# Two H3 convolution layers and two MLP layers on one core: the skip weight D added by TensorE, one more channel group turned by DMA, LayerNorm statistics swapped between VectorE and ScalarE, and a new order of the front

## The chip, the cores and the metric

The kernel runs on one core of a Trainium2 chip. A core has five engines with their own in-order instruction queues: TensorE (PE in the profile; PEld is its weight load), VectorE (DVE), ScalarE (ACT), GpSimd (POOL) and SyncE (SP), which here issues nearly all DMAs. They meet only at semaphores. Matmuls write to PSUM; VectorE and ScalarE copy PSUM to SBUF (an *evacuation*), while GpSimd works on SBUF alone. The metric is the device time of one execution in microseconds. Before the change the median of three runs was 256.5 us (255.91 to 257.84).

## The reference, cut to what matters

```python
def _A_ref(q, k, v, shift_k, ssm_k, ssm_D):          # S = 2048 tokens, D = 512 channels
    k_shift = sum(k_pad[:, t:t + S, :] * shift_k[:, ks - 1 - t] for t in range(4))   # four taps
    kv = k_shift * v
    y = irfft(rfft(kv, 2 * S) * rfft(ssm_k, 2 * S))[:, :S, :].astype(bf16)  # long causal convolution
    return q * (y + kv * ssm_D)                      # D: a skip weight for each channel
def _B_ref(x, w1, b1, w2, b2):                       # MLP 512 -> 1376 -> 512
    return gelu(layernorm(x) @ w1 + b1) @ w2 + b2

x = A_q
x = x + _A_ref(layernorm(x), ...);  x = x + _B_ref(layernorm(x), ...)
x = x + _A_ref(layernorm(x), ...);  x = x + _B_ref(layernorm(x), ...)
```

Both A layers use the same k, v and kernels, and only their gate q differs, so the convolution `y + kv * D` is computed once and used twice. Adding D to the first sample of the convolution kernel gives the same result as `kv * D`: this is how the kernel does it.

## The kernel before, in words

The program has a **front** (to about 98 us in the profile), which computes the convolution for all tokens and the first token group's gate, and an **MLP part** of eight rounds (two layers of four token groups), each a product with w1 and Gelu (`mm1`, lines 704 and 706) and a product with w2 (`mm2`, line 738).

The front is a list of pieces. Each piece is planned with `plan.add` and names its dependences, and the string ORDER at the head of the file fixes the order by hand: a word such as `U2S0.P02` is a piece, its engine (P TensorE, A ScalarE, D VectorE, G GpSimd, S SyncE) and the buffers that it takes. Each engine runs its pieces in the order of that string. There are four PSUM buffers p0 to p3 (of 1024 f32 columns each), three SBUF buffers ZT, three xb and three T.

The pieces, by channel group cc = 0 to 3 of 128 channels (a trailing `e` is the evacuation of the piece before it):

- **lk, lv, lK, lX, lW, lM, lx0, lx1, lx**: loads of k, v, the convolution kernel, tables, and of the input x. lx0 and lx1 are token groups 0 and 1 for LayerNorm 0; lx is all of x once more, into the place of v.
- **kT**: k turned by TensorE (line 441). **dg**: diagonal matrices of the tap weights (line 435), which the matmuls **kv** (line 524) use to apply the four taps for cc 0 to 2; **kvm** multiplies by v on VectorE (line 530). For cc = 3 the taps are **kg** and **ka** on GpSimd (lines 455 to 462, about 4 us each), and kgm.
- **kd**: D is added to the first sample of the convolution kernel, `Kd[:, :, 0] += Dz`, on VectorE (line 393), once for each half of it.
- **KS, K2** (lines 400 and 413): the transform of the convolution kernel in two stages of 16 pieces each.
- **US** (line 325): first transform stage of u = kv, four pieces for each cc. **UT**: u is turned between its stages, in two halves, by 16 transposes on TensorE and an evacuation (line 357), or by a DMA transpose (line 304), as the string `UT` says for each cc.
- **X, T, V** (lines 558, 573, 582): 16 rounds of second stage, product with the kernel's transform (VectorE, 128x2048) and first inverse stage. A T needs KSW, a rearranged copy of K2's result that the loads **sa** and **sb** make.
- **Z, TC, TD** (lines 629, 617): the result turned again, by DMA for cc 0 and 1 and by TensorE for cc 2 and 3. **Y** (line 649): last inverse stage for each token group. **g0, h0, p0, b0** (lines 674, 259, 271, 276): gate, statistics, root and scaling for group 0's three units (tokens 0, 1 and 2 to 3 of the group). **LT0** (line 657): its first unit turned for mm1.
- **s0, s1, s02**: LayerNorm 0's statistics for groups 0 and 1 (on VectorE lines 259 to 268, on ScalarE lines 487 to 490), their scale on GpSimd, and group 0's scaling (line 508).

Behind the front, PSUM's place is taken over by the tiles `ph` (four, where p0 and p1 were) and `po` (four, where p2 and p3 were) of the MLP part.

Of the kernel before, what the change touches and what calls it, by code (L numbers as in the profile page):

```python
# [11 lines left out]
ALU = mybir.AluOpType  # L12
# [18 lines left out]
T20.D0 X21e.A U3S1.P1 U0T0.P2 lx.S U3S1e.A T10.D1 X13.P30 U3S3e.A V20.P10 U0T0e.D X13e.A U3T0.S X23.P01 T21.D2
U0T1.P2 V20e.A T13.D0 X00.P32 X23e.A V10.P11 U0T1e.D X00e.A V21.P0 V10e.A T23.D1 X01.P30 V13.P2 V21e.A T00.D2
# [93 lines left out]
def kernel(ctx: ExitStack, tc: tile.TileContext, A_q, A_k, A_v, A_shift_k, A_ssm_k, A_ssm_D,  # L126
                 B_x, B_w1, B_b1, B_w2, B_b2, out):
    nc = tc.nc
    P = 128
    _, S, D = A_q.shape  # L130
    F = B_w1.shape[1]
# [3 lines left out]
    FT = (F + P - 1) // P  # L135
    FL = F - (FT - 1) * P
# [98 lines left out]
    def evac(eng, dst, src):  # L235
        if eng == "A":
            nc.scalar.activation(dst, src, AF.Copy)  # L237
        else:
            nc.vector.tensor_copy(dst, src)  # L239
# [587 lines left out]
```

## Time and profile before

| what | us |
|---|---|
| median of three runs | 256.5 |
| the profiled execution's own time | 256.8 |
| its span (all that the profile shows) | 255.1 |
| TensorE busy in the span | 236.8 |
| VectorE / ScalarE busy in the span | 174.5 / 146.1 |
| GpSimd busy in the span | 54.5 |

The profile gives one execution. Time that lies outside the span (256.8 - 255.1 = 1.7 us) is not seen in it. In its rows, the first number is the start in us from the span's start, the second the length; `x4` means four instructions merged into a row; in brackets stand the idle time of the engine just before, and what ended it. Busy shares are averages over stages that have different limits, so each stage is read for itself. Merged rows overlap a little, since an instruction starts before the one ahead of it has drained: a copy shown with 1.22 us follows the last one after 1.16.

### The profile page before, as it was taken

The page shows a single profiled execution, that of the slowest core. Times are in us where ns is not written, and L with a number is a line of the kernel's source. Part 1 is how long each engine was busy: PE and PEld are TensorE (multiplying, and loading weights), DVE is VectorE, ACT ScalarE, POOL GpSimd, SP SyncE. Part 2 cuts the span into 40 slices and gives each one's busy share as a digit, 9 for nine tenths or more (in the row PEclk, how much of TensorE's full clock was granted, in tenths as well). Part 3 has the DMA queues.
Part 4 walks back from the last instruction along what each step waited for, and adds up shares of the span by engine and source line. Part 5 has one row for each costly group of instructions (what it writes and reads, how often), then busy time and mean ns, then how long its engine had stood idle before and what let it go on. Part 6 is the DMA issues. An engine that isn't in the chain of part 4 may idle for free.

```text
span 255.1 us, 5088 instructions
## 1 busy us (share of the span) xinstructions
PE 236.8 (93%) x2084; PEld 146.3 (57%) x2084; DVE 174.5 (68%) x321; ACT 146.1 (57%) x210; POOL 54.5 (21%) x52
## 2 busy tenths in 40 slices
PE   1898479999999999999999999999999999999995
PEld 0698446889989857854444444444444444444443
DVE  0345988899999897787889989886866863022022
ACT  3698388899999799921821721722712712812810
POOL 2499999310000011011110111110110110000000
PEclk9999975899999999999999999999999999999999
DMA  5999994199967898004040401304006006002001
GB/s 132 382 334 167 222 442 180 76 320 321 312 135 103 148 237 288 3 0 82 5 82 0 78 6 20 62 0 82 4 1 165 0 11 157 0 14 71 1 20 63
DMA packets 53040, 30.15 MB, mean 118 GB/s; under 512 B 46642, under 2 KB 50456, under 8 KB 51736
## 3 DMA queue, kind: packets, MB, share of 16 engines
q1 hardware_dynamic: 52864, 29.73, 43.5%
q8 instruction: 16, 0.26, 0.4%
q10 hardware_dynamic: 152, 0.09, 0.1%
q14 instruction: 8, 0.07, 0.1%
HBM read 16.71 MB, written 2.10 MB: 74 GB/s over the span
## 4 chain that ended last, share of the span: by engine, by line
PE 72%; DVE 12%; DMA 7%; issue 4%; ACT 2%; SPq 2%; ACTq 0%; DVEq 0%
PE po L738 30%; PE ph L704 29%; DMA arena<-in_A_v_dram 4%; DVE T L573 4%; DVE arena L239 3%; PE p L325 2%; PE p L357 2%; PE p L649 2%; DVE arena L393 2%; DMA arena<-in_A_ssm_D_dram 2%; PE p L400 2%; PE p L413 2%; PE p L524 1%; DVE ZT L239 1%; DMA arena<-ZT 1%
## 5 line engine op out<-in xcount | busy, mean ns | idle before, releaser
L706 ACT ACTIVATE arena<-ph,B 128x512 bf16<-128x512 f32 (+5 forms) x110 | 63.7, 604 | 81.1 <-PE ph L704 81.0
L704 PE MATMUL ph<-arena 128*128 128x512 bf16 (+4 forms) x440 | 78.5, 336 | 0.1
L738 PE MATMUL po<-arena 128*128 128x512 bf16 (+2 forms) x363 | 77.4, 373 | 0.0
L704 PEld LDWEIGHTS <-arena 128*128 128x128 bf16 (+1 forms) x440 | 40.4, 100 | 37.2 <-DMA arena<-in_B_w_dram 0.4
L738 PEld LDWEIGHTS <-arena 128*128 128x128 bf16 (+1 forms) x363 | 35.4, 98 | 40.5
L743 DVE TENSOR_TENSOR arena<-po,arena 128x512 bf16<-128x512 f32 (+1 forms) x33 | 21.5, 673 | 43.6 <-PE po L738 43.6
L237 ACT ACTIVATE arena<-p 128x1024 bf16<-128x1024 f32 (+5 forms) x38 | 37.8, 1071 | 10.1 <-PE p L441 3.9
L271 POOL TENSOR_TENSOR lrsm<-lrsm,mhalf 128x4 f32<-128x4 f32 (+2 forms) x10 | 8.9, 885 | 95.9 <-DVE lrsm L265 95.9
L237 ACT ACTIVATE ZT<-p 128x1024 bf16<-128x1024 f32 (+1 forms) x22 | 22.0, 1055 | 2.5 <-PE p L325 2.5
L259 DVE BATCH_NORM_STATS2 lstm<-arena 128x6 f32<-128x512 bf16 x32 | 19.9, 681 | 0.2
L573 DVE TENSOR_TENSOR T<-xb,arena 128x2048 bf16<-128x2048 bf16 (+1 forms) x17 | 18.7, 1159 | 0.0
L239 DVE CAST arena<-p 128x1024 bf16<-128x1024 f32 x15 | 17.7, 1223 | 1.4 <-PE p L400 0.9
L582 PE MATMUL p<-arena,T 128*128 128x128 bf16 x256 | 16.5, 219 | 1.0 <-DVE arena L239 0.4
L271 POOL TENSOR_TENSOR lrsg<-lrsg,mhalf 128x4 f32<-128x4 f32 x8 | 8.1, 1014 | 40.2 <-DVE lrsg L268 40.1
L237 ACT ACTIVATE xb<-p 128x1024 bf16<-128x1024 f32 x15 | 16.1, 1165 | 0.1
L582 PEld LDWEIGHTS <-T 128*128 128x128 bf16 x256 | 14.9, 98 | 1.6 <-issue 1.3
L455 POOL TENSOR_TENSOR T<-arena,SK 128x2048 bf16<-128x2048 bf16 (+3 forms) x4 | 14.9, 3740 | 3.8 <-ACT arena L237 3.7
L259 DVE BATCH_NORM_STATS2 lstg<-arena 128x6 f32<-128x512 bf16 x24 | 14.8, 679 | 0.0
L276 DVE TENSOR_SCALAR arena<-arena,lmvg,lrsg 128x512 bf16<-128x512 bf16 x28 | 9.7, 409 | 6.7 <-POOL lrsg L271 6.7
L239 DVE COPY arena<-p 128x2048 bf16<-128x2048 bf16 (+3 forms) x10 | 10.5, 1049 | 4.4 <-issue 3.0
L276 DVE TENSOR_SCALAR arena<-arena,lmvm,lrsm 128x512 bf16<-128x512 bf16 x32 | 11.2, 409 | 2.3 <-POOL lrsm L271 2.3
L524 PE MATMUL p<-DG,arena 128*128 128x128 bf16 x192 | 11.4, 219 | 1.2 <-ACT ZT L237 0.9
(73 smaller groups left out, 226.8 us busy)
## 6 DMA issues: line engine op xcount, KB each, us to landing
arena<-arena SPq DMA_DIRECT2D x8, 512.0 KB, 4.2
arena<-in_A_k_dram SPq DMA_DIRECT2D x4, 512.0 KB, 6.2
arena<-in_A_v_dram SPq DMA_DIRECT2D x2, 1024.0 KB, 9.6
arena<-in_A_ssm_k_dram SPq DMA_DIRECT2D x4, 512.0 KB, 7.9
arena<-tabM SPq DMA_DIRECT2D x1, 2048.0 KB, 12.1
arena<-in_A_q_dram SPq DMA_DIRECT2D x1, 2048.0 KB, 8.2
out_dram<-arena SPq DMA_DIRECT2D x15, 128.0 KB, 1.7
arena<-in_B_w_dram SPq DMA_DIRECT2D x1, 1376.0 KB, 6.5
```

The source lines that it names most:

```text
L237: nc.scalar.activation(dst, src, AF.Copy)
L239: nc.vector.tensor_copy(dst, src)
L259: nc.vector.bn_stats(self.st[:, i, 0, :], x_t[:, GT * g + i, :] if src is None else src[:, i, :])
L271: nc.gpsimd.tensor_tensor(self.rs[:, a:b], self.rs[:, a:b], mhalf[:, a:b], ALU.pow)
L276: nc.vector.tensor_scalar(out=dst[:, i, :], in0=xs, scalar1=self.mv[:, i, 0:1], scalar2=self.rs[:, i:i + 1], op0=ALU.subtract, op1=ALU.mult)
L455: nc.gpsimd.tensor_tensor(m[:, t:NT, :], kn[:, 0:NT - t, c3], sk(t, NT - t), ALU.mult)
L573: eng.tensor_tensor(view(Tb[it["slot"]["T"]], [2, n, CW]), x2, kk, ALU.mult)
L582: nc.tensor.matmul(o[:, i, :], T[:, r, i, :], Mt[:, ka + i, 1 - r, :], start=r == 0, stop=r == 1)
L704: nc.tensor.matmul(o.rearrange("p (i t) -> p i t", t=P), W1t[:, ct, ft * P:ft * P + m], lt[:, a:b, ct, :], start=ct == 0, stop=ct == CT - 1)
L706: nc.scalar.activation(hT[0:m, ft, a * P:b * P], o, AF.Gelu_apprx_tanh, bias=B1[0:m, ft:ft + 1])
L738: nc.tensor.matmul(po[:, a:b], hT[0:m, ft, i * P:(i + 1) * P], W2t[0:m, ft, a:b], start=ft == 0, stop=ft == FT - 1)
L743: nc.vector.tensor_tensor(xs, po[:, a:b], xs, ALU.add)
```

## The change

1. **D by TensorE.** kd becomes two matmuls with the identity, `Kd[:, :, 0]` and `Dz` summed in PSUM, and an evacuation of 128x64 back into Kd, which the new order gives to ScalarE.
2. **u of cc = 2 turned by DMA** (`UT` is `PPXX`): U2T0 and U2T1 become DMA transposes.
3. **x in four loads** lr0 to lr3, one for each token group, that wait for all US and for X30 and X31; the first gate waits for lr0 only. lr1 to lr3 stand among the weight loads at the front's end. The weight loads no longer wait for all T: w1 for the first two T of each cc, the others for the second and third.
4. **GpSimd's taps** wait until all three dg are made.
5. **LayerNorm 0**: group 0's scaling s02 may run on ScalarE alone (it did). In the new order group 0's statistics are on VectorE and group 1's on ScalarE; before it was the other way round.
6. **A new ORDER**, with new planned costs. The planned costs have no effect on the program: the order is written out.

```diff
@@ ORDER (only two of its lines)
-lSK.S lk1.S lsT.S lk3.S lk0.S lk2.S bSK.P0 lh1.S bSKe.A lh113.S lx0.S kT1.P1 lv0.S sF.G lv1.S dg0.D dg2.D
+lSK.S lk1.S lk3.S lk2.S lk0.S lsT.S lh1.S lx0.S bSK.P0 lh113.S bSKe.D kT1.P1 lx1.S lv1.S kT3.P2 kT1e.A lv0.S
...
-    UT = "PPPX"
+    UT = "PPXX"
...
-                kd = plan.add(f"kd{c}", {"G": 300, "D": 130}, lK[c * NK // 8], lambda it, sl=sl: (
-                    nc.vector if it["eng"] == "D" else nc.gpsimd).tensor_tensor(Kd[:, sl, 0], Kd[:, sl, 0], Dz[:, sl], ALU.add))
+                def mms(o, sl=sl):
+                    nc.tensor.matmul(o, IDt[:], Kd[:, sl, 0], start=True, stop=False)
+                    nc.tensor.matmul(o, IDt[:], Dz[:, sl], start=False, stop=True)
+                _, kd = mm_evac(f"kd{c}", 120, lK[c * NK // 8], mms, [P // NK], lambda sl=sl: Kd[:, sl, 0])
...
-            kg.append(plan.add(f"kg{t}", {"G": 4650 if t else 4100}, kg[-1:] if t else lk + lS[2:] + [bSK], lambda it, t=t: tap(t)))
+            kg.append(plan.add(f"kg{t}", {"G": 4650 if t else 4100}, kg[-1:] if t else lk + lS[2:] + [bSK] + dg, lambda it, t=t: tap(t)))
...
-            return s0, plan.add("s02", {"D": 1350, "A": 2200}, [s1], apply) if n == 0 else s1
+            return s0, plan.add("s02", {"A": 2900}, [s1], apply) if n == 0 else s1
...
-        lx = load("lx", x_t[:], q_d.rearrange(TOK, p=P), 2 ** 21, USp)
...
-        w1 = load("w1", W1t[:], B_w1.rearrange("(ct p) f -> p ct f", p=P), 1376 << 10, sum(Tcc, []))
-        wd = sum(Tcc, [])
+        lx = [load(f"lr{g}", x_t[:, GT * g:GT * g + GT, :], xd[:, GT * g:GT * g + GT, :], 2 ** 19, USp + Xcc[3][:2],
+                   rank=2 if g else 0) for g in range(4)]
+        w1 = load("w1", W1t[:], B_w1.rearrange("(ct p) f -> p ct f", p=P), 1376 << 10, sum((t[0:2] for t in Tcc), []))
+        wd, we = sum(Tcc, []), sum((t[1:3] for t in Tcc), [])
...
-            ga = plan.add(f"g0{a}", {"D": 1190 if m == 2 else 930}, [y, s2, lx], gate, free=yf)
+            ga = plan.add(f"g0{a}", {"D": 1190 if m == 2 else 930}, [y, s2, lx[0]], gate, free=yf)
```

What the new order does on the engines, at three places. First VectorE, from the first product with v (line 530, now 532) on to the evacuations of KS (`128x64x8x2`). `p0` to `p3` are the PSUM buffers; line 393 is the addition of D. Before:

```order
L530 TENSOR_TENSOR arena_64<-p2_121,arena_64 128x8x128
L239 CAST ZT0_95<-p1_120 128x4x8x32
L393 TENSOR_TENSOR arena_64<-arena_64,Dz_72 128x64
L530 TENSOR_TENSOR arena_64<-p3_122,arena_64 128x8x128
L239 CAST arena_64<-p1_120 128x64x8x2
```

After, from the evacuation of the last kT on (line 259 and the two rows behind it are group 0's statistics):

```order
L239 COPY arena_64<-p0_119 128x4x3x128
L259 BN_STATS lstg0_104<-arena_64 128x6 x4
L263 BN_AGGR lmvg0_105<-lstg0_104 128x2 x4
L268 TENSOR_SCALAR lrsg0_106<-lmvg0_105 128x4
L532 TENSOR_TENSOR arena_64<-p1_120,arena_64 128x8x128
L532 TENSOR_TENSOR arena_64<-p2_121,arena_64 128x8x128
L532 TENSOR_TENSOR arena_64<-p3_122,arena_64 128x8x128
L532 TENSOR_TENSOR arena_64<-p0_119,arena_64 128x8x128
L239 CAST ZT0_95<-p1_120 128x4x8x32
L532 TENSOR_TENSOR arena_64<-p2_121,arena_64 128x8x128
```

The addition of D has left VectorE, and the statistics of group 0 stand ahead of the first product with v.

Second SyncE's queue, from the last copies of KSW (`64x4096`) to the weights; line 304 is the turning of u (ZT1 holds cc = 2, ZT0 cc = 3), line 632 a Z. This is what stands there now:

```order
L301 DMA arena_64<-arena_64 64x4096 x6
L304 DMA_TRANSPOSE arena_64<-ZT1_96 128x16x128
L304 DMA_TRANSPOSE arena_64<-ZT0_95 128x16x128
L304 DMA_TRANSPOSE arena_64<-ZT1_96 128x16x128
L632 DMA_TRANSPOSE arena_64<-arena_64 128x8x128
L304 DMA_TRANSPOSE arena_64<-ZT0_95 128x16x128
L632 DMA_TRANSPOSE arena_64<-arena_64 128x8x128
L301 DMA arena_64<-in_A_q_dram 128x2048
L632 DMA_TRANSPOSE arena_64<-ZT2_97 128x8x128
```

Before, the load of all of x (`128x8192`) followed KSW's copies, then the two turns of cc = 3, and then all Z. Now there are four turns of u with a Z (Z01) ahead of the last one, and x's first quarter stands behind the second Z.

Third VectorE at the end of the front, from the evacuation TC2e (`128x8x256`) to the scaling of group 0's last unit (line 276, x2), behind which the MLP part has it. Before:

```order
L239 COPY arena_64<-p0_119 128x8x256
L276 TENSOR_SCALAR arena_64<-arena_64,lmvm0_111,lrsm0_112 128x512
L674 TENSOR_TENSOR arena_64<-arena_64 128x1024
L675 TENSOR_TENSOR arena_64<-arena_64 128x1024
L276 TENSOR_SCALAR arena_64<-arena_64,lmvm0_111,lrsm0_112 128x512
L239 COPY arena_64<-p0_119 128x512
L259 BN_STATS lstm0_110<-arena_64 128x6 x2
L263 BN_AGGR lmvm0_111<-lstm0_110 128x2 x2
L265 TENSOR_SCALAR lrsm0_112<-lmvm0_111 128x2
L239 CAST arena_64<-p2_121 128x1024
```

After, the last ten rows of that stretch:

```order
L678 TENSOR_TENSOR arena_64<-arena_64 128x1024
L259 BN_STATS lstm0_110<-arena_64 128x6
L263 BN_AGGR lmvm0_111<-lstm0_110 128x2
L265 TENSOR_SCALAR lrsm0_112<-lmvm0_111 128x1
L239 CAST arena_64<-p3_122 128x1024
L276 TENSOR_SCALAR arena_64<-arena_64,lmvm0_111,lrsm0_112 128x512
L259 BN_STATS lstm0_110<-arena_64 128x6 x2
L263 BN_AGGR lmvm0_111<-lstm0_110 128x2 x2
L265 TENSOR_SCALAR lrsm0_112<-lmvm0_111 128x2
L239 CAST arena_64<-p1_120 128x1024
```

VectorE now evacuates two of the last Y there (Y22 from p3 and, last of all, Y12 from p1), where before it was one (Y32 from p2), and LT0 has gone to ScalarE. By the program's semaphores, the first tile of mm1 takes p0's place and the second p1's: before, the second tile waited for ScalarE's evacuation of Y20 out of p1, and now it waits for VectorE's evacuation of Y12.

54 lines of the change are left out of this document (27 added, 27 removed).

## The prediction, made before the changed kernel was run

> **What bounds the kernel now.** I read the busy time by stage first, then the rows in order of time. Columns: stretch, its length, busy us (and instructions) of PE, PEld, DVE, ACT, POOL, then granted clock, DMA share, GB/s.
>
> ```profile
> 60.00:70.00 10.00, 9.91 (x163) 9.59 (x161) 10.00 (x10) 10.00 (x12) 0.00 (x0) 1.00 1.07 295
> 70.00:80.00 10.00, 9.20 (x159) 8.84 (x157) 10.00 (x10) 10.00 (x12) 0.00 (x0) 1.00 0.45 98
> 110.00:255.00 145.00, 142.15 (x669) 65.86 (x667) 88.88 (x212) 52.90 (x78) 13.09 (x13) 1.00 0.18 41
> ```
>
> Behind 110 us TensorE is busy for 142 of 145 us: the MLP part is bound by it, and the change touches nothing there. From 60 to 80 it is VectorE and ScalarE, both at 10.00 of 10, that bound the front, while TensorE has gaps. So a us taken from VectorE ahead of the last T counts; one taken from TensorE there does not. I follow one **anchor**, the first matmul of the product with w2 (109.37, below). The 145.7 us behind it stay, and so do the 1.7 us outside the span: time = anchor + 147.4 us (256.8 for this execution, 0.3 above the median).
>
> **Part 1: to VectorE's first evacuation of K2.** What the added D costs now:
>
> ```profile
> 25.95 3.61 POOL L455 TENSOR_TENSOR T<-arena,SK 128x1792 bf16<-128x1792 bf16 x1
> 26.35 3.52 DVE L393 TENSOR_TENSOR arena<-arena,Dz 128x64 bf16<-128x64 bf16 x1
> 29.93 0.64 PE L400 MATMUL p<-Ft,arena 32*128 32x64 bf16 x32 [2.79 <-DVE arena L393]
> ```
> ```profile
> 34.40 3.37 POOL L455 TENSOR_TENSOR T<-arena,SK 128x1664 bf16<-128x1664 bf16 x1
> 36.35 1.73 DVE L393 TENSOR_TENSOR arena<-arena,Dz 128x64 bf16<-128x64 bf16 x1
> 38.13 0.78 PE L400 MATMUL p<-Ft,arena 32*128 32x64 bf16 x48 [1.58 <-DVE arena L393]
> ```
>
> 64 elements take VectorE 3.52 and 1.73 us, and each ends 0.3 us behind the GpSimd tap that began before it: the addition is held by the tap. TensorE waits 2.79 and 1.58 us for it. The product with v at 15.32 (line 530, one operand in PSUM, below) runs beside a tap at 1.22 and is not held. In the new kernel TensorE adds D and ScalarE evacuates 128x64. No row shows that one:
>
> ```profile
> L237 ACT ACTIVATE arena<-p 128x256 bf16<-128x256 bf16 x2 | 0.8, 383 | 0.4 <-PE p L617 0.3
> L488 ACT ACTIVATE as<-as 128x4 f32<-128x4 f32 x1 | 0.2, 207 | 0.0
> L487 ACT ACTIVATE arena<-arena 128x512 bf16<-128x512 bf16 x4 | 2.5, 630 | 0.2
> L490 ACT ACTIVATE arena<-arena,as 128x512 bf16<-128x512 bf16 x4 | 2.9, 722 | 0.1
> ```
>
> 128x256 took 0.38 us and 128x4 0.21, so 0.2 to 0.4, say 0.3, on ScalarE, and beside it TensorE's two matmuls of 64 columns, under 0.2. Both waits go, 4.4 us of TensorE's. What is late next is VectorE's own queue, so I count from its start:
>
> ```profile
> 11.18 0.98 PEld L441 LDWEIGHTS <-arena 128*128 128x128 bf16 x12 [0.39 <-DMA arena<-in_A_k_dram]
> 11.31 7.95 POOL L455 TENSOR_TENSOR T<-arena,SK 128x2048 bf16<-128x2048 bf16 x2 [3.67 <-ACT arena L237]
> 12.66 3.75 PE L524 MATMUL p<-DG,arena 128*128 128x128 bf16 x64 [0.33 <-ACT arena L237]
> 15.32 1.22 DVE L530 TENSOR_TENSOR arena<-p,arena 128x1024 bf16<-128x1024 f32 x1 [1.93 <-DMA arena<-in_A_v_dram]
> 17.91 2.36 DVE L530 TENSOR_TENSOR arena<-p,arena 128x1024 bf16<-128x1024 f32 x2 [1.36 <-DMA arena<-in_A_v_dram]
> ```
> ```profile
> 10.00:16.00 6.00, 5.54 (x82) 5.11 (x81) 1.63 (x2) 5.72 (x12) 4.69 (x2) 1.00 1.04 407
> ```
>
> kv starts at 12.66 and takes 1.88 each (3.75 for two); the last k landed at 11.2. The little load behind dg now stands behind all four loads of k, and kT0's evacuation stands behind dg0 on VectorE: about 11.5 landed, then cast (0.2), dg0 (0.7) and the copy (1.0) give kv at 13.4, and the four kv ahead of kvm20 end at 20.9. v used to land for 15.32 and 17.91; lx1 now goes ahead, 0.52 MB at 407 GB/s or 1.3 us, so 16.6 and 19.2, hidden behind kv. From 20.9 VectorE has six pieces of 1.23 (three products with v, three US), eight KS at 1.16 and two US, 19.1 us: it is free for K2 at **40.0**. ScalarE has two dg to 14.3, group 1's statistics (lines 487 to 490: 2.5 + 2.9 and the small steps, 6.6 us) to 20.9 and group 0's scaling (2.9) to 23.8, and then waits for kd0 at 25.6: nothing, with a cover of 1.8 us; what goes beyond it delays KS one for one.
>
> Two terms are added. (a) Group 0's statistics now run on VectorE from 13.4 to 16.5, while the first tap, which waits for dg1, runs from about 14.3 to 18.4. Their last step is an SBUF-to-SBUF operation as line 393 was. If held, VectorE begins with v at 18.5 and is 1.2 late at kvm20: 0 to 1.2, I take 0.6. (b) The clock:
>
> ```profile
> 28.93:32.34 3.41, 1.94 (x77) 1.00 0.87 304
> 32.34:35.76 3.42, 3.42 (x44) 0.50 1.08 447
> 35.76:39.17 3.42, 1.57 (x82) 1.00 0.99 422
> 39.17:42.58 3.41, 3.28 (x83) 0.50 0.59 240
> 42.58:46.00 3.42, 3.42 (x24) 0.50 0.00 0
> ```
>
> (Columns: busy PE, granted clock, DMA share, GB/s.) Both times a stretch with only 1.6 to 1.9 us of TensorE work, mostly KS matmuls of 32 rows, was followed by half clock; and a stretch full of KS (39.17) did not end it. KS stays, so I expect half clock again at K2's start, where three US and three K2 must run before VectorE's first one: 0 to 1.7, I take 1.4. Sum: 40.0 + 0.6 + 1.4 = **42.0**, before 46.38.
>
> The Trainium skill (TensorE: Matmul & The Clock Gate, What's actually happening) says that the clock halves after an idle window of some 3.4 us. This trace halves it after windows that were half busy, so the measurement decides; by the rule (b) would be nothing, and the time 1.4 us less.
>
> **Part 2: to the last T.**
>
> ```profile
> L573 DVE TENSOR_TENSOR T<-xb,arena 128x2048 bf16<-128x2048 bf16 x15 | 17.5, 1222 | 0.0
> L239 DVE CAST arena<-p 128x1024 bf16<-128x1024 f32 x6 | 7.1, 1219 | 0.5 <-PE p L413 0.5
> L239 DVE COPY arena<-p 128x2048 bf16<-128x2048 bf16 x5 | 6.1, 1223 | 0.8 <-PE p L357 0.4 <-issue 0.3
> L239 DVE CAST ZT<-p 128x1024 bf16<-128x1024 f32 x3 | 3.7, 1222 | 0.0
> L259 DVE BATCH_NORM_STATS2 lstg<-T 128x6 f32<-128x512 bf16 x4 | 2.5, 679 | 0.0
> ```
> ```profile
> 46.38 1.23 DVE L239 CAST arena<-p 128x1024 bf16<-128x1024 f32 x1 [0.34 <-PE p L413]
> 47.75 4.62 DVE L239 CAST arena<-p 128x1024 bf16<-128x1024 f32 x4 [0.15 <-PE p L413]
> ```
> ```profile
> 79.98 4.70 DVE L573 TENSOR_TENSOR T<-xb,arena 128x2048 bf16<-128x2048 bf16 x5
> ```
>
> From 46.38 to 84.68 (79.98 + 4.70) VectorE spends 38.3 us without a real gap. In the new order group 1's statistics leave (3.1 with their small steps), and of five 128x2048 copies of UT four stay (-1.2); it gets six K2 instead of five (+1.2) and six other casts instead of four (+2.4). Sum -0.7. Laying the 16 rounds out with these durations leaves it 0.4 us of new waits: 42.0 + 38.0 = **80.0**, before 84.68. **So the front's gain is 4.7 us**, and most of it comes from D, not from the turning: the 32 transposes that TensorE saves lie beside a saturated VectorE.
>
> The turning moves to SyncE:
>
> ```profile
> L304 SPq DMA_TRANSPOSE arena<-ZT x2: 3849/4944/6039, 63.6 to 69.7; - x2
> ```
> ```profile
> 87.91 2.70 SPq L629 DMA_TRANSPOSE arena<-ZT  x2
> ```
>
> One half took 3.8 to 6.0 us of the queue, waits for the loads ahead included. At 2.7 (two Z, together as much data, take 2.70) all four end by 70; X32, the tightest, comes at 74.5: cover 4 us. x's four loads and the weights come 10 us ahead of use or more: nothing. w1's earlier release is not used, since it stands behind all Z.
>
> **Part 3: from the last T to the anchor**, before 109.37 - 84.68 = 24.7 us.
>
> ```profile
> 96.87 0.42 DVE L239 COPY arena<-p 128x512 bf16<-128x512 bf16 x1
> 98.81 1.22 DVE L239 CAST arena<-p 128x1024 bf16<-128x1024 f32 x1
> ```
> ```profile
> 97.91 2.11 PE L704 MATMUL ph<-arena 128*128 128x128 bf16 x32
> 100.09 0.38 PE L657 MATMUL po<-IDt,arena 128*128 128x128 bf16 x4
> 109.37 2.97 PE L738 MATMUL po<-arena 128*128 128x512 bf16 x13
> ```
>
> Now VectorE's last evacuation (Y32, out of p2) ends at 100.05, 15.4 behind the last T, and mm1 hardly notices: it has done 8 of 11 tiles of its first unit by then. After the change mm1's *second* tile needs p1, which VectorE empties last (Y12). VectorE's list there gains an evacuation (1.2) and a small one (0.3) and loses LT0's (0.4), but it also loses some 0.9 of waits: Y12 ends at 15.6. TensorE, done with Y12 at about 13, stands still for 2.5 us, and 7 tiles that were done before (0.264 each, 2.11 for 8) come afterwards: 0.2 + 1.85, and 0.15, an estimate, for one more handoff between TensorE and ScalarE. **The tail loses 2.2 us.** Such a pause can halve the clock again (above: half-busy windows): 0 to 1.7, I take 0.8 as it depends on where the window falls.
>
> Sum: anchor 109.4 - 4.7 + 2.2 + 0.8 = 107.7, time **255.1 us**.
>
> **Rivals.** *B, the clock stays full at K2 and at the pause, and nothing of the statistics is held*: for it, much of the KS stage is mixed with US. S is 40.0, so 40.0 + 38.0 - 84.7 + 2.2 = -4.5: **252.3**. *C, the tap holds all of group 0's statistics*, not only their last step: two of four run before 14.3, the rest from 18.4, and VectorE begins with v at 20.4 instead of 16.6. kvm20 is 3.2 late instead of 0.6: 255.1 + 2.6 = **257.7**, slower than before. For it: 3.52 us on line 393. Against it: an operation with one SBUF operand is none that the trace shows held.
> The Trainium skill (GPSIMD Engine Reference, Key points) has GpSimd contend with VectorE operations that have two SBUF inputs or run in a 2-port mode. Line 393 agrees with 3.52 us; statistics with one input would fall under it only in such a mode, which no run here shows.
> *D, SyncE's queue becomes the bound*: at 5 us for each half (the mean of 9.95 for two) U3's second half, which stands behind a Z, lands at 78 instead of 70, and X32 stands still for 3.5 us, and the last T with it: **258.6**; it decides from 3.5 us a half on. *E, TensorE goes on waiting for D*, now for ScalarE's evacuation of it, which stands behind group 0's scaling: the cover is 1.8 us, and if ScalarE is 3 us later than laid out, KS is 1.2 late: **256.3**.
>
> **Chances.** Forecast 0.52, B 0.25, C 0.09, D 0.11, E 0.03. A measurement of this kernel can tell about 1% (2.6 us) from no change. Faster by more: B and a little of the forecast's range, 0.28. Slower by more needs C or D with the clock's full price (1.7 instead of 0.8) or with each other: 0.13. Within: 0.59. The forecast's own range is 253.3 to 257.3 (terms a and b and the pause at their ends). Range: from B, 252.0, to D with the full clock price, 259.4.
>
> **What would show it.** Line 393 gone and no TensorE wait ahead of KS; VectorE's first K2 evacuation at 42 (B: 40, C: 44.6) and the last T at 80; half clock at K2's start; statistics of group 0 that end by 16.5 or 18.6; a pause of 2 to 3 us in mm1 right behind its first tile, ended by VectorE, and the anchor 27 to 28 us behind the last T. The prediction is wrong if mm1 runs without that pause, or if VectorE has gaps of microseconds between K2 and the last T.

## The result, and the profile after

The changed kernel takes **259.2 us** (median of seven runs, 258.13 to 260.03), the kernel before 256.8 in the same comparison: 1.0085 times as long, with a 95% interval of 1.0063 to 1.0106. The prediction was 255.1, range 252.0 to 259.4: forecast a little faster, measured slower by 0.85%. The profiled execution took 258.1 us, the least of the seven, with a span of 256.4. The ratios here leave out executions more than 1.5% above the fastest of the same kernel: three of the six of warm_ks, one of u2_by_pe, and one of the kernel before beside stats_first_only.

Three points divide the span as the prediction did:

| | before | predicted | after (profiled) |
|---|---|---|---|
| VectorE's first evacuation of K2 begins | 46.38 | 42.0 | 44.94 |
| last T ends | 84.68 | 80.0 | 82.27 |
| anchor: first product with w2 | 109.37 | 107.7 | 110.47 |
| from the last T to the anchor | 24.69 | 27.7 | 28.20 |

So the end of the front lost what was forecast (3.5 us instead of 3.0), and the front gained 2.4 us instead of 4.7. The front's loss can be read at its start, in VectorE's rows in order of time (start, length, line, operation, out<-in):

```profile
10.89 0.96 DVE L239 COPY arena<-p 128x1536 bf16<-128x1536 bf16 x1 [7.47 <-PE p L443]
11.76 4.43 DVE L437 TENSOR_SCALAR DG<-IDt,sF 128x128 bf16<-128x128 bf16 x4
16.11 0.94 DVE L239 COPY arena<-p 128x1536 bf16<-128x1536 bf16 x1
16.98 2.45 DVE L259 BATCH_NORM_STATS2 lstg<-arena 128x6 f32<-128x512 bf16 x4
...
19.75 0.17 DVE L268 TENSOR_SCALAR lrsg<-lmvg 128x4 f32<-128x4 f32 x1
19.86 1.22 DVE L532 TENSOR_TENSOR arena<-p,arena 128x1024 bf16<-128x1024 f32 x1
...
24.95 1.22 DVE L532 TENSOR_TENSOR arena<-p,arena 128x1024 bf16<-128x1024 f32 x1 [0.56 <-PE p L526]
```

The four small operations that make the diagonal dg0 take 4.43 us together. The view of that line alone gives each one's shortest, median and longest duration in ns:

```profile
L437 DVE TENSOR_SCALAR DG<-IDt,sF x4: 241/242/3942, 11.8 to 15.9; 128x128 bf16<-128x128 bf16 x4
```

Three took 0.24 us, one 3.94. On GpSimd, in the same stretch:

```profile
11.33 0.20 POOL L382 CAST sF<-sT 128x16 f32<-128x16 bf16 x1 [3.87 <-DMA sT<-in_A_shift_k_dram]
11.56 4.09 POOL L457 TENSOR_TENSOR T<-arena,SK 128x2048 bf16<-128x2048 bf16 x1
```

The first tap began at 11.56, right behind the cast, and **ahead of** the diagonals for which the change was to hold it. It ends at 15.65 (11.56 + 4.09). The four operations begin at 11.76, and the last of them starts at 15.9, so the long one ends with the tap. TensorE waits for dg0:

```profile
15.76 9.15 PE L526 MATMUL p<-DG,arena 128*128 128x128 bf16 x128 [3.32 <-DVE DG L437]
```

and all that VectorE has behind dg0 (the last kT, the statistics, the products with v) comes as much later. Before, VectorE made all three diagonals from 7.67 on, since the load behind them landed earlier, and the first tap began only at 11.31:

```profile
7.67 2.04 DVE L435 TENSOR_SCALAR DG<-IDt,sF 128x128 bf16<-128x128 bf16 x12 [7.67 <-POOL sF L382]
```

The end of the front is as the prediction had it. TensorE's rows (with its wait in brackets), VectorE's last evacuation, and the clock in stretches of 2 us (busy PE, granted clock, DMA share, GB/s):

```profile
94.90 0.39 PE L707 MATMUL ph<-arena 128*128 128x128 bf16 x4
98.04 3.14 PE L707 MATMUL ph<-arena 128*128 128x128 bf16 x28 [2.75 <-DVE arena L239]
```
```profile
96.76 1.23 DVE L239 CAST arena<-p 128x1024 bf16<-128x1024 f32 x1
```
```profile
96.00:98.00 2.00, 0.00 (x0) 1.00 1.07 377
98.00:100.00 2.00, 1.96 (x19) 0.50 1.09 375
100.00:102.00 2.00, 2.00 (x27) 0.65 0.47 172
102.00:104.00 2.00, 1.99 (x33) 1.00 0.02 6
```

One tile of mm1, then 2.75 us of nothing until Y12 has left p1, then half clock for about 3.4 us.

### The profile page after: what moved, and what is told of

Its sections match the earlier page's. It is cut to its first block, busy times and chain, and to the rows that moved or that the text cites. A ratio compares the mean times of both kernels' runs of the same rounds, so it can differ in the third digit from the quotient of the medians.

```text
span 256.4 us, 5044 instructions
## 1 busy us (share of the span) xinstructions
PE 237.8 (93%) x2056; PEld 148.1 (58%) x2056; DVE 178.8 (70%) x318; ACT 141.1 (55%) x211; POOL 54.6 (21%) x52
## 4 chain that ended last, share of the span: by engine, by line
PE 76%; DVE 13%; DMA 5%; ACT 2%; issue 2%; SPq 1%; DVEq 0%; ACTq 0%
PE ph L707 30%; PE po L741 30%; DVE arena L239 5%; PE p L526 4%; DMA arena<-in_A_k_dram 2%; DMA arena<-ZT 2%; PE p L325 2%; PE p L583 2%; DVE ZT L239 2%; PE p L620 2%; PE p L402 2%; DVE T L574 2%; DVE DG L437 2%; PE p L415 1%; DVE arena L532 1%
## 5 line engine op out<-in xcount | busy, mean ns | idle before, releaser
L707 PE MATMUL ph<-arena 128*128 128x512 bf16 (+4 forms) x440 | 80.0, 342 | 2.9 <-DVE arena L239 2.8
L707 PEld LDWEIGHTS <-arena 128*128 128x128 bf16 (+1 forms) x440 | 41.9, 103 | 39.8 <-issue 2.9
L741 PEld LDWEIGHTS <-arena 128*128 128x128 bf16 (+1 forms) x363 | 35.5, 98 | 40.5
L746 DVE TENSOR_TENSOR arena<-po,arena 128x512 bf16<-128x512 f32 (+1 forms) x33 | 21.5, 672 | 43.5 <-PE po L741 43.5
L237 ACT ACTIVATE arena<-p 128x1024 bf16<-128x1024 f32 (+7 forms) x36 | 33.1, 996 | 13.3 <-PE p L394 5.6
L239 DVE CAST arena<-p 128x1024 bf16<-128x1024 f32 x17 | 20.0, 1216 | 1.1 <-PE p L402 0.7
L237 ACT ACTIVATE ZT<-p 128x1024 bf16<-128x1024 f32 (+1 forms) x19 | 18.8, 1034 | 1.1 <-PE p L325 1.1
L259 DVE BATCH_NORM_STATS2 lstg<-arena 128x6 f32<-128x512 bf16 x28 | 17.2, 676 | 0.0
L526 PE MATMUL p<-DG,arena 128*128 128x128 bf16 x192 | 13.1, 234 | 3.3 <-DVE DG L437 3.3
L239 DVE COPY arena<-p 128x2048 bf16<-128x2048 bf16 (+3 forms) x10 | 9.9, 1006 | 8.8 <-PE p L443 7.5
L526 PEld LDWEIGHTS <-arena 128*128 128x128 bf16 x192 | 12.5, 106 | 3.8 <-DVE DG L437 3.6
L237 ACT ACTIVATE xb<-p 128x1024 bf16<-128x1024 f32 x14 | 14.4, 1075 | 0.2 <-PE p L559 0.2
```

The costliest lines, as they stand in the source:

```text
L259: nc.vector.bn_stats(self.st[:, i, 0, :], x_t[:, GT * g + i, :] if src is None else src[:, i, :])
L526: nc.tensor.matmul(o[:, i, :], w, DG[:, cc, t, :], start=t == 0, stop=t == KS - 1)
L707: nc.tensor.matmul(o.rearrange("p (i t) -> p i t", t=P), W1t[:, ct, ft * P:ft * P + m], lt[:, a:b, ct, :], start=ct == 0, stop=ct == CT - 1)
L741: nc.tensor.matmul(po[:, a:b], hT[0:m, ft, i * P:(i + 1) * P], W2t[0:m, ft, a:b], start=ft == 0, stop=ft == FT - 1)
L746: nc.vector.tensor_tensor(xs, po[:, a:b], xs, ALU.add)
```

## The experiments

All times below are compared with the kernel before on the same chip; a median is of 4 to 12 executions (hold_forms: one). K2 is the start of VectorE's first evacuation of K2 in the profiled execution, T the end of the last T, A the anchor.

| run | median us | ratio to before (95%) | K2 | T | A | A - T |
|---|---|---|---|---|---|---|
| after | 259.2 | 1.0085 (1.0063 to 1.0106) | 44.94 | 82.27 | 110.47 | 28.2 |
| tap_waits | 256.9 | 0.9973 (0.9951 to 0.9995) | 44.63 | 81.90 | 109.81 | 27.9 |
| tail_slots | 256.3 | 0.9952 (0.9927 to 0.9976) | 46.85 | 84.08 | 109.14 | 25.1 |
| both_fixes | 253.7 | 0.9853 (0.9818 to 0.9888) | 44.84 | 82.11 | 107.19 | 25.1 |
| before_d_pe | 254.9 | 0.9885 (0.9851 to 0.9918) | 44.33 | 82.75 | 107.45 | 24.7 |
| stats_first | 252.5 | 0.9817 (0.9783 to 0.9851) | 42.65 | 79.88 | 104.93 | 25.1 |
| diag_act | 252.3 | 0.9807 (0.9780 to 0.9834) | 41.50 | 79.24 | 104.32 | 25.1 |
| stats_first_only | 255.2 | 0.9933 (0.9906 to 0.9961) | 42.37 | 79.58 | 107.48 | 27.9 |
| d_on_dve | 257.9 | 1.0024 (1.0005 to 1.0043) | 47.71 | 85.04 | 110.11 | 25.1 |
| u2_by_pe | 257.2 | 0.9996 (0.9964 to 1.0029) | 42.12 | 84.08 | 109.12 | 25.0 |
| v_first | 254.9 | 0.9897 (0.9870 to 0.9924) | 44.98 | 82.27 | 107.37 | 25.1 |
| warm_ks (three of six in the ratio) | 256.7 | 0.9874 (0.9832 to 0.9916) | 48.58 | 85.87 | 110.91 | 25.0 |
| hold_forms | 258.9 | none (one execution) | 48.95 | 86.16 | 111.21 | 25.1 |

The kernel after and tail_slots have the same front, and their K2 stands at 44.94 and 46.85: one execution differs from the next by up to 2 us there. So causes are read from the rows, and prices from the ratios: a difference of 0.01 between two of them is 2.6 us.

### tap_waits: the tap made to wait for the diagonals

```diff
+            if not t:
+                nc.gpsimd.tensor_copy(ksum[:, 0, 0:CK], DG[:, :, KS - 1, 0])
             nc.gpsimd.tensor_tensor(m[:, t:NT, :], kn[:, 0:NT - t, c3], sk(t, NT - t), ALU.mult)
```

> The kernel after, with one 128x3 copy on GpSimd ahead of the first tap that reads the last diagonal of each group, so that the tap really waits for all three. Theory W (in the kernel after nothing made the tap wait: it began at 11.56 beside VectorE's four diagonals, held one of them for 3.94 us, and the product with the taps began at 15.76 where the prediction had 13.4): the four diagonals take about 1 us, the products kv begin at 12.7 to 13.4, VectorE's first evacuation of K2 comes at 42.0 to 42.6 instead of 44.94, and the time falls by 2.4 to 2.9 us from the kernel after, to about 256.5. If the tap, which then runs from 14.1 to 18.1, holds group 0's last statistics step, that step ends at 18.2 and not by 16.5. Rival T (something else made VectorE late there, and the tap only lay beside it): the diagonals stay long, and the time stays within 1 us of the kernel after. Rival Q (the queue of transposes is at its limit already, since X32 waited 0.7 us for one in the kernel after): the first evacuation of K2 comes at 42.3, but the last T moves by less than 1.5 us.

The ratio fell by 0.0112, or 2.9 us. VectorE and GpSimd:

```profile
11.85 0.74 DVE L437 TENSOR_SCALAR DG<-IDt,sF 128x128 bf16<-128x128 bf16 x4 [0.35 <-POOL sF L382]
...
16.15 2.63 DVE L268 TENSOR_SCALAR lrsg<-lmvg 128x4 f32<-128x4 f32 x1
```
```profile
14.64 4.12 POOL L459 TENSOR_TENSOR T<-arena,SK 128x2048 bf16<-128x2048 bf16 x1
```

The diagonals take 0.74 us instead of 4.43: the tap was the cause, and rival T falls. But the tap, moved, now holds the next operation of that kind: four numbers in each partition take 2.63 us, to 18.78, when the tap ends at 18.76. Of the 3.7 us won, VectorE keeps 1.2 at first (it begins with v at 18.70 instead of 19.86) and, since it no longer waits for kv, 2.9 at kvm20 (22.1, the last of four products that take 4.60 us from 18.70, instead of 24.95). Even so K2 moved by only 0.3 between the two profiled executions, not by the 2.4 to 2.9 expected: in this one the clock was 0.70 from 22.10 to 25.50 and 0.80 from there to 28.90, where the kernel after had 1.00, and the 32 matmuls of kv at 22.68 took 2.93 us instead of 1.95. A longer queue of transposes (rival Q) isn't what took it: from K2 to the last T it took 37.27 us, as in the kernel after (37.33).

### tail_slots: two places in PSUM exchanged

```diff
-Y20.P2 ... Y12.P1
+Y20.P1 ... Y12.P2
```

> The kernel after, with the places in PSUM of the last two products of Y exchanged: Y20 (evacuated by ScalarE) in p1, Y12 (evacuated last, by VectorE) in p2, as no more than a renaming. Theory P (mm1's second tile waits 2.75 us for VectorE's last evacuation out of p1, and half clock follows the pause): the wait goes, the clock stays full there, and the time falls by 2.5 to 3.5 us, to about 256.2. Rival L (mm1 is bound by VectorE's last scalings and the turning of the other token units anyway, so the pause only moves behind mm1's first unit): the wait shows up at the first turning of the next unit, and the time falls by less than 1 us.

```profile
96.69 2.20 PE L707 MATMUL ph<-arena 128*128 128x128 bf16 x32
99.86 0.38 PE L660 MATMUL po<-IDt,arena 128*128 128x128 bf16 x4 [0.98 <-DVE arena L239]
```

TensorE now does eight tiles of mm1 in a row; 0.98 us of a wait is left behind them. From the last T to the anchor it takes 25.1 us instead of 28.2, with the clock at 1.00 throughout. The ratio falls by 0.0133, or 3.4 us. Theory P holds: nearly all of the loss at the front's end (3.1 of 3.5 us) was which of two evacuations stood in which place.

### both_fixes

> The two edits of the runs before it together. If the two costs lie one behind the other, their gains add up: 2.4 to 2.9 and 2.5 to 3.5 us from the kernel after, which makes 253 to 254, and 1.0 to 1.5% faster than the kernel before. If the transposes or the clock take one of them back, the sum is smaller by what shows up as a new wait at X32 or as half clock.

0.0232 under the kernel after, where the two runs before it make 0.0112 + 0.0133 = 0.0245: the gains add up, within their intervals, to 6.0 us.

### before_d_pe: D by TensorE as the only part

```diff
-U0S0e.A kd0.D U0S3.P2 kvm20.D
+U0S0e.A kd0.P0 U0S3.P2 kd0e.A kvm20.D
...
-KS01.P2 kd4.D KS50.P0
+kd4.P1 KS01.P2 kd4e.A KS50.P0
```

(on top of the kernel before, with the two matmuls of the change)

> The kernel before, with D alone added by TensorE: two matmuls with the identity and an evacuation of 128x64 by ScalarE in place of VectorE's addition, both times, and nothing else moved. Theory D (the two additions, held 3.52 and 1.73 us by the taps, delay KS and with it K2): TensorE's waits of 2.79 and 1.58 us go, VectorE's first evacuation of K2 comes 2.5 to 4 us ahead of 46.38, and the time falls by the same, to 253 to 254.5. Rival V (VectorE is the bound of that stretch and only the 5 us held count in part; or half clock and the loads of the tables take its place): the first evacuation of K2 comes less than 1.5 us earlier.

The ratio of 0.9885 is worth 3.0 us, and K2 came 2.05 earlier in the profiled execution: by K2 between the two theories (2.5 and more, less than 1.5), by the ratio within theory D, though the median of 254.9 is above its 253 to 254.5. TensorE's waits for D are gone, but in the old order it is then TensorE that VectorE waits for, up to 1.71 us in front of KS.

### stats_first: GpSimd's scale of group 0 ahead of its first tap

```diff
-kv01.P1 kg0.G s10.A kv11.P2 kvm01.D kv00.P3 s01.G kvm11.D
+kv01.P1 s01.G kg0.G s10.A kv11.P2 kvm01.D kv00.P3 kvm11.D
```

(on top of tail_slots; no copy of a diagonal)

> The kernel after with the exchanged places of Y20 and Y12, and with GpSimd's scale of group 0 (s01, three small steps that need VectorE's statistics) moved ahead of its first tap; nothing else, and no copy of a diagonal. GpSimd then waits for the statistics' last step, and the diagonals are long made by then. Theory W (the tap holds only VectorE's operations that lie beside it with both ends in SBUF: with the copy it held the last statistics step for 2.63 us): neither the diagonals nor the last step are held, that step ends at 16.5 and not at 18.8, VectorE begins with v at 16.6 to 17.0 instead of 18.7 to 19.0, kvm20 ends 1.8 us earlier than with both fixes, and the time falls by 1.5 to 2.0 us from theirs, to 251.7 to 252.2. Rival Q (half clock in KS and at the start of K2 takes it back, as in the shown execution with the waiting tap, where kvm20 came 1.6 us earlier and the first evacuation of K2 0.3): less than 0.7 us from both fixes.

```profile
11.98 0.73 DVE L437 TENSOR_SCALAR DG<-IDt,sF 128x128 bf16<-128x128 bf16 x4
...
16.27 0.17 DVE L268 TENSOR_SCALAR lrsg<-lmvg 128x4 f32<-128x4 f32 x1
17.11 2.36 DVE L532 TENSOR_TENSOR arena<-p,arena 128x1024 bf16<-128x1024 f32 x2 [0.67 <-DMA arena<-in_A_v_dram]
20.45 2.36 DVE L532 TENSOR_TENSOR arena<-p,arena 128x1024 bf16<-128x1024 f32 x2 [0.98 <-DMA arena<-in_A_v_dram]
```
```profile
18.11 7.95 POOL L457 TENSOR_TENSOR T<-arena,SK 128x2048 bf16<-128x2048 bf16 x2
```

The tap begins at 18.11, and neither small operation is held: 0.73 and 0.17 us. What VectorE waits for now is the loads of v. K2 at 42.65, the last T at 79.88, the time 252.5: 0.9 us under both fixes by the ratios, the intervals of which overlap, so this settles neither theory W (1.5 to 2.0) nor rival Q (less than 0.7); and 3.5 us (0.0135) under tail_slots, which differs in this alone.

### diag_act: all diagonals on ScalarE

```diff
-lK01.S dg2.A lK00.S dg0.D kT0e.D dg1.A
+lK01.S dg0.A lK00.S dg1.A kT0e.D dg2.A
```

> The kernel after with the exchanged places of Y20 and Y12, and all three diagonals on ScalarE, in the order 0, 1, 2; the tap begins at 11.6 as in the kernel after. Theory W: ScalarE is not held by the tap, the products kv begin at 12.8, and VectorE's statistics end at 15.7, their last step at the end of the tap at the latest; VectorE begins with v at 16 to 17 and the time is within 0.7 us of the run with the statistics first, 252 to 252.7. Rival A (ScalarE's 1.2 us more, ahead of group 1's statistics and of group 0's scaling, delay D's evacuation and KS): 253.5 or more.

```profile
11.60 3.62 ACT L435 ACTIVATE DG<-IDt,sF 128x128 bf16<-128x128 bf16 x12 [0.55 <-POOL sF L382]
```
```profile
11.60 4.13 POOL L457 TENSOR_TENSOR T<-arena,SK 128x2048 bf16<-128x2048 bf16 x1
```
```profile
13.34 2.46 DVE L259 BATCH_NORM_STATS2 lstg<-arena 128x6 f32<-128x512 bf16 x4
```

The tap lies where it lay in the kernel after. ScalarE makes twelve diagonal blocks beside it at 0.30 us each (eight took 2.44 us beside the tap in the kernel after, and 2.44 in stats_first without one), and VectorE's statistics run beside it too and take 2.46 us, the same as without a tap. 252.3 us: two ways round the hold, one time. It is the fastest kernel measured, equal to stats_first within their intervals.

### stats_first_only: the tap behind the statistics as the only edit

The same move of s01 as the only edit of the kernel after.

> The kernel after with GpSimd's scale of group 0 ahead of its first tap as the only edit: neither the diagonals nor the last statistics step lie beside a tap, and the places in PSUM at the end of the front are as the change made them. This is the program for which the prediction's own steps were worked out (the tap behind the diagonals). If its other terms hold, the first evacuation of K2 comes at 41.5 to 42.7, the last T ends at 79.2 to 80.3, TensorE pauses for 2.5 to 2.9 us behind mm1's first tile, the first product with w2 comes 27.7 to 28.3 us behind the last T, and the time is 255.1 to 256.2, 3 to 4 us under the kernel after. Rival: the two costs are not additive (the pause falls into another place of the clock, or the front's gain is waited away at the end): 257 or more.

**255.2 us**: K2 at 42.37, the last T at 79.58, the anchor 27.9 behind it, TensorE's pause 2.80. All six numbers lie in the expected bounds. But this is not quite the program of the prediction: there the tap runs beside the statistics' last step (as in tap_waits), here it begins behind it, at 17.62.

### d_on_dve: D on VectorE again, in the new order

```diff
-kd0.P2 U2S1.P0 kd0e.A lX.S
+kd0.D U2S1.P0 lX.S
...
-kd4.P3 U0S1.P0 kd4e.A KS41.P3
+kd4.D U0S1.P0 KS41.P3
```

(on top of stats_first)

> The run with the statistics first, with D added on VectorE again, as in the kernel before, at the place of the two evacuations in the order. Theory D (the two additions are held by GpSimd's operations until these end, and VectorE's chain sets K2's start): each is held for 1 to 4 us, the first evacuation of K2 comes 2.5 to 5 us later than 42.65, and the time rises by as much, to 255 to 257.5: D is then worth as much as, or more than, the whole front's gain of 4.7 in the prediction. Rival K (D alone is worth 2.3 us, as in the kernel before, since there is slack behind it): the time rises by 2.3 us or less.

```profile
28.07 3.13 DVE L393 TENSOR_TENSOR arena<-arena,Dz 128x64 bf16<-128x64 bf16 x1
...
36.73 2.94 DVE L393 TENSOR_TENSOR arena<-arena,Dz 128x64 bf16<-128x64 bf16 x1
```

Each ends 0.3 us behind a sum on GpSimd (these end at 30.90 and 39.37). Held for 3.13 and 2.94 us, K2 5.1 us later, the time 5.3 us longer (0.0207): theory D, a little above its bounds. In the new order nearly every held us counts; of the 5.2 us in the old one before_d_pe returned 3.0. Rival K falls.

### u2_by_pe: u of cc = 2 turned by TensorE again

```diff
-    UT = "PPXX"
+    UT = "PPPX"
...
-X12.P21 V00e.A U3T0.S V02e.D X11.P30
+U2T0.P2 V00e.A U3T0.S V02e.D U2T0e.D X12.P21 X11.P30
```

(the second half in the same manner ahead of X20; on top of stats_first)

> The run with the statistics first, with u of cc = 2 turned by TensorE again: 32 transposes, and two copies of 128x2048 by VectorE among the T of cc 0 and 1. Theory S (VectorE and ScalarE are saturated there, so the turning by DMA was worth its evacuations): first evacuation of K2 to last T grows from 37.3 by 1.2 to 2.3 us, and so does the time, to 253 to 254. Rival H (the transposes' queue holds X32 by as much as the copies cost): the wait of X32 for a transpose goes, and the time is within 0.7 us.

4.6 us longer (0.0179), all of it between K2 and the last T (42.0 instead of 37.2 us): more than theory S had. Two copies of 1.16 us on VectorE make 2.3; the rest are waits that the copies set off:

```profile
63.54 1.05 PE L559 MATMUL p<-arena,Wt 128*128 128x128 bf16 x16 [1.81 <-DVE arena L239]
70.12 0.61 PE L559 MATMUL p<-arena,Wt 128*128 128x128 bf16 x8 [1.38 <-DVE arena L239]
```

X waits until VectorE has come round, and VectorE then waits for TensorE (0.97 us at 65.59, 0.89 at 68.84; in stats_first it is busy for all of 60 to 70). The place was chosen for this run and the order not tuned to it, so 4.6 is best read as an upper bound of what the turning by DMA is worth. Rival H falls: no X gained.

### v_first: x's second group loaded behind v

```diff
-kT1.P1 lx1.S lv1.S kT3.P2 kT1e.A lv0.S
+kT1.P1 lv1.S lv0.S kT3.P2 kT1e.A lx1.S
```

(on top of stats_first)

> The run with the statistics first, with the load of token group 1 (lx1) moved behind both loads of v on SyncE's queue. Theory V (the two waits of VectorE for v, 0.67 and 0.98 us in the run with the statistics first, are what is left of the new order of the loads, which the prediction had hidden): v lands 1.2 and 2.0 us earlier or more, both waits go, kvm20 ends 1.0 to 1.6 us earlier, and the time is 0.8 to 1.5 us under the run with the statistics first. Rival Q (half clock in KS and at the start of K2, or the phase in which it falls, takes it back) or L (group 1's statistics on ScalarE, 3.6 us later, delay D's evacuation): within 0.5 us of it, or above.

```profile
20.70 0.63 ACT L489 ACTIVATE arena<-T 128x512 bf16<-128x512 bf16 x1 [6.73 <-DMA T<-in_A_q_dram]
...
30.03 0.43 ACT L237 ACTIVATE arena<-p 128x64 bf16<-128x64 f32 x1
```
```profile
30.51 2.76 PE L402 MATMUL p<-Ft,arena 32*128 32x64 bf16 x96 [3.21 <-ACT arena L237]
```

VectorE's waits for v went, and the run was 2.1 us slower (0.0080): group 1 of x landed at 20.7, its statistics and group 0's scaling kept ScalarE to 30.0, and D's evacuation, which stands behind them, let KS begin at 30.5 instead of 27.5. Rival L, and the mechanism of the prediction's rival E: in the kernel after ScalarE sat idle for 5.4 us ahead of that evacuation, so it cost nothing there.

### warm_ks: TensorE kept busy through KS

```diff
                 def mms(o, c=c, g=g):
+                    for e in range(4):
+                        nc.tensor.matmul(o[:, e // 2, 2 * (e % 2):2 * (e % 2) + 2, :], IDt[:], IDt[:], start=True, stop=True)
```

(on top of stats_first)

> The same, and each of the 16 KS pieces begins with four 128x128 matmuls of the identity into the place in PSUM that its own matmuls overwrite: about 0.23 us more of TensorE's work at full clock for each, with 128 rows. Theory C (half clock in KS and at the start of K2 follows from windows in which TensorE is half busy with matmuls of 32 rows, and it costs what the prediction's term b had): the granted clock stays at 1.00 for most of the stretch from 29 to 46, the first evacuation of K2 comes 1.0 to 1.7 us earlier, and the time falls by as much from the run with the statistics first. Rival N (VectorE and ScalarE are the bound of that stretch at either clock, or the clock does not ask what the rows are): the clock stays as it was or the time moves by less than 0.5 us, or rises by the added work.

The clock in the profiled execution (259.1 us), and below it that of stats_first (busy PE, granted clock, DMA share, GB/s):

```profile
28.93:32.34 3.41, 3.30 (x88) 1.00 1.20 185
32.34:35.76 3.42, 3.42 (x94) 1.00 0.92 381
35.76:39.17 3.41, 2.38 (x56) 1.00 1.03 430
39.17:42.58 3.41, 3.41 (x75) 0.62 0.92 389
```
```profile
32.34:35.76 3.42, 3.07 (x84) 0.50 1.02 407
35.76:39.17 3.41, 3.14 (x67) 0.50 1.04 442
```

With the added matmuls KS ran at full clock for nearly 10 us in this execution, until a stretch with 2.38 us of work was followed by half clock. Three of the six executions had a mean clock of 1.00 in all (252.7, 254.5 and 254.8 us), against 0.973 to 0.980 in the six of stats_first: so half clock there does depend on what TensorE does. The edit adds both rows and work, and which of the two the clock follows is open. It did not pay: the three are 1.5 us slower than stats_first by the ratios (0.0057). The other three, the profiled one among them, had 0.97 to 0.98 and took 258.7 to 260.4; what parts them from the first is not shown. What full clock gave and what the added work took can't be told apart here; no part of the first is left over, which speaks for rival N.

### hold_forms: which operations a tap holds

Six small operations on VectorE, the results of which nothing uses, on top of stats_first (one execution, 258.9 us, 6.4 above stats_first's median): a copy bf16 to bf16, a product f32 with a constant, a product of two f32, a copy bf16 to f32, a product of two bf16, and statistics.

> The run with the statistics first, with six small extra operations on VectorE that nothing else uses, spread over the stretch from 19 to 40 us in which GpSimd runs one tap or sum behind the other (3.4 to 4.1 us each): a copy of 128x64 bf16 to bf16, a product of 128x16 f32 with a constant, a product of two f32 operands, a copy of 128x64 bf16 to f32, a product of two bf16 operands, and statistics of 128x128. Theory W (held are operations with both ends in SBUF, other than statistics, up to the end of GpSimd's operation): the bf16 product of two operands and the f32 product with a constant last 0.3 to 4 us, up to the end of a tap; the statistics take 0.2 to 0.3. The two copies and the f32 product of two operands tell what sets it: the number of operands in SBUF (then the copies take 0.1 to 0.2), or both ends in SBUF (then all are held). Each held operation adds its wait to VectorE's chain, so the time rises by 4 to 10 us.

```profile
18.91 3.10 DVE L453 COPY pB<-IDt 128x64 bf16<-128x64 bf16 x1
...
25.33 0.52 DVE L454 TENSOR_SCALAR pF<-sF 128x16 f32<-128x16 f32 x1
...
30.42 0.17 DVE L455 TENSOR_TENSOR pF<-sF 128x16 f32<-128x16 f32 x1
...
32.77 1.35 DVE L456 CAST pF<-IDt 128x64 f32<-128x64 bf16 x1
...
36.31 2.58 DVE L457 TENSOR_TENSOR pB<-IDt,Dz 128x64 bf16<-128x64 bf16 x1
...
43.33 0.28 DVE L458 BATCH_NORM_STATS2 pF<-IDt 128x6 f32<-128x128 bf16 x1
```
```profile
17.87 7.94 POOL L467 TENSOR_TENSOR T<-arena,SK 128x2048 bf16<-128x2048 bf16 x2
...
30.43 3.64 POOL L467 TENSOR_TENSOR T<-arena,SK 128x1792 bf16<-128x1792 bf16 x1
...
34.78 4.05 POOL L474 TENSOR_TENSOR T<-T,T 128x2048 bf16<-128x2048 bf16 x1
...
43.25 4.06 POOL L474 TENSOR_TENSOR T<-T,T 128x2048 bf16<-128x2048 bf16 x1
```

The copy ends at 22.0 and the cast to f32 at 34.1, the f32 product with a constant at 25.85, the bf16 product at 38.9: each within 0.1 us of the end of a GpSimd operation (34.07, 25.8 and 38.83; the first of the two merged taps ends half way through its row, at about 21.9). The statistics at 43.33 lie inside one and take 0.28. The product of two f32 began in the gap ahead of a GpSimd operation (30.42 against 30.43) and tells nothing. So one operand is enough to be held.

The rule fits a page of the Trainium skill (SBUF — State Buffer, Who interferes with whom): copies, casts and products with a constant in the modes that use both ports, and, beside a GpSimd operation that reads SBUF, operations with two inputs there, find the port pair taken until GpSimd's operation ends. The four held rows agree (1.35 to 3.10 us for the three of 64 elements), though no row shows the mode in which an operation ran; the page does not name the statistics, which ran free here.

## Why the prediction was wrong

**The step that failed** is in part 1: "the first tap, which waits for dg1, runs from about 14.3 to 18.4", which followed the change's own description. It does not wait. The edit adds the diagonals to the tap's list of dependences, but `plan.write` follows ORDER word by word and never reads that list; a wait in the program comes from the data and places that an instruction reads or writes, and the tap reads k and the weights (`kn`, `SK`), never `DG`. The program built without that edit has the same instructions on every engine. So this part of the change does nothing, and the same holds of the waits that part 3 of the change lists for x's quarters and the weights. The tap began at 11.56, and what the prediction knew of line 393 (held until the tap ends) happened to dg0, at the head of everything (3.94 us for one operation that takes 0.24): kv began at 15.76, not 13.4, and kvm20 at 24.95, not 21.5. That is 3.4 us, and the prediction missed K2 by 2.9. That the change might not do what it says was not among the rivals.

The other steps, with what the runs say of each:

- **D's two additions were the front's main cost**: right, and more than was said. d_on_dve prices them at 5.3 us in the new order; the front with the hold gone gains 4.8 in all (84.68 - 79.88, stats_first). In the old order they were worth 3.0.
- **ScalarE's evacuation of D**, taken at 0.3: 0.46 us. It was covered, as forecast; v_first shows what it costs when it isn't.
- **Term (a)**, the last statistics step held by the tap: not in the kernel after, where the tap had ended by then (0.17 us). With the tap where the prediction put it (tap_waits) it was held for 2.63 us, and kvm20 began at 22.1: the upper end of the bounds (20.9 + 1.2).
- **Rival C**, all of the statistics held: refuted. In diag_act they ran beside the tap at their usual 0.6 us.
- **v hidden behind kv**: not quite. In stats_first_only VectorE waited 0.52 and 1.69 us for it and began at 16.47 and 20.51, where 16.6 and 19.2 were taken; this took the place of term (a), and the sum came out at 42.37 by other terms than those written.
- **Term (b)**, 1.4 us for half clock at K2's start: from kvm20 to K2, 19.1 us of VectorE's work took 20.0 in the kernel after and 20.7 in stats_first_only, 0.9 and 1.6 more, waits of every kind included. The size was right; warm_ks leaves open how much of it is the clock. Rival B, full clock at K2 and at the pause, did not come: the clock of the kernel after was 0.50 from 35.76 to 42.58, and 0.50 behind the pause.
- **Part 2**, 38.0: 37.3, 0.7 less. That the turning gives little of the front's gain was badly put: undone at one place it cost 4.6 us, through the copies and the waits that they set off. And **the cover of 4 us at X32** was not there (below).
- **Part 3**: right in mechanism, place and size. A pause of 2.5 us behind mm1's first tile was forecast, 2.75 measured, ended by VectorE; half clock followed. The tail took 28.2 us against 27.7, and tail_slots returned 3.1 of the 3.5 lost.

On the cover at X32, the chain of the kernel after has (start, length, what):

```profile
70.88 6.15 DMA arena<-ZT
...
77.07 0.62 PE p L559 x8
```

and SyncE's queue and stats_first:

```profile
70.88 1.96 SPq L304 DMA_TRANSPOSE arena<-ZT  x1
```
```profile
74.60 0.62 PE L559 MATMUL p<-arena,Wt 128*128 128x128 bf16 x8 [0.17 <-DMA arena<-ZT]
```

This turn landed 6.15 us after its issue. The prediction took the 2.7 us for which the queue is occupied as the whole, and had the last one done by 70; it landed at 77.0, and TensorE waited 0.3 us for it. In stats_first X32 came at 74.60, where the prediction had it (74.5), and waited 0.17 us: the cover was used up there too. Rival D was close, but its stop of 3.5 us did not come.

One sum of the prediction does not come out: with terms (a), (b) and the pause at their ends, the forecast's own range is 252.3 to 256.9, not 253.3 to 257.3.

With the failed step made true (tap_waits) the ratio is 0.9973, or 256.1 us from 256.8. That is 2.9 us of the 3.9 by which the forecast of 255.1 (0.9934) was missed; 0.6 more is term (a) at its end, with which the sum makes 255.7. stats_first_only comes to the forecast's number, 255.2 us, but in part by luck: there term (a) is nothing, and waits for v stand in its place. The change as it stands pays 3.9 us (1.0085 against 0.9933) for the tap beside the diagonals, and 3.4 (tail_slots) for the exchanged places; without both it would be 1.8 to 1.9% faster than the kernel before.

## What to carry to other kernels

A dependence in a planner's list is not a wait: before a hold is counted on, look at what the held instruction reads and writes, since in this program only that made the semaphore. On a kernel with long GpSimd operations, list what VectorE runs beside them: here a copy, cast, product or sum inside SBUF cost what was left of the GpSimd operation, however small it is (4 numbers per partition: 2.63 us), while evacuations from PSUM (1.22 us), statistics (0.6) and the diagonals on ScalarE (0.30) cost nothing extra. And where a later stage takes over buffers, let the buffer that its second tile needs be the one that comes free early: two exchanged places were worth 3.4 us.

## What the runs showed of the hardware that was not expected

- VectorE operations with **one** operand in SBUF were held by GpSimd too: 3.94 us (product with a constant, 128x128), 3.10 (copy of 64 elements), 1.35 (cast to f32), 2.63 (4 elements of f32).
- Statistics were not, at 128x512 (0.6 us each beside a tap) and 128x128 (0.28).
- A turn of 128x2048 by DMA landed 6.15 us after its issue, while SyncE's queue was occupied for 1.96 us of it.
- Busy time alone did not tell the granted clock: stretches of stats_first with 3.07 and 3.14 us of TensorE work out of 3.42, mostly of 32 rows, ran at 0.50; in warm_ks, with matmuls of 128 rows added, a stretch with 2.38 ran at 1.00. Whether the rows or the amount of work set it is open.
